# Linear attention on one core: q transposed by the DMA, k and q^T sharing their elementwise work, z from one-column products, two banks for kv

## Chip, cores, metric

One core of one Trainium2 chip. The metric is the device time of one execution in microseconds (us). "Span" is the time between the first and the last instruction of the profiled execution; it is about 2 us shorter than the device time. PE is the tensor engine, DVE the vector engine, ACT the scalar engine, POOL the GpSimd engine, and SP the engine that issues the DMAs.

## The reference

```python
B, H, S, D = 1, 32, 2048, 128          # q, k, v: bf16, normal * 0.05
phi_q = where(q > 0, q + 1, exp(q)) + 1e-6
phi_k = where(k > 0, k + 1, exp(k)) + 1e-6
kv  = einsum("bhsd,bhse->bhde", phi_k, v)
z   = einsum("bhsd->bhd", phi_k)
num = einsum("bhqd,bhde->bhqe", phi_q, kv)
den = einsum("bhqd,bhd->bhq", phi_q, z)[..., None] + 1e-6
out = num / den
```

Both kernels split phi(x) into two parts, min(exp(x), 1) + 1e-6 and max(x, 0), and let PE add them: two products instead of one. Each head is 512 KB of q, of k, of v and of output.

## The kernel before

All work is written as one list of operations per engine. Every engine runs its own list strictly in order and waits on semaphores for results of the others. So the order in which the helper functions are called in the main loop *is* the order on each engine. The parts that matter (cut):

```python
def T(h):      # PE: 16 transposes of q into PSUM, (L243)
def ek(h):     # ACT: exp of k                    (L190)
def eq(h):     # ACT: exp of q^T from PSUM        (L194)
def rqa(h):    # ACT: max(q^T, 0), half or all    (L202)
def rqb(h):    # DVE: the other half              (L207)
def emrk(h):   # DVE: min of exp(k) (L220), max of k (L222)
def emq(h):    # DVE: min of exp(q^T)             (L227)
def v1(h):     # POOL: copy v next to a column of ones (L236)
def kv(h):     # PE: 32 products of 129 columns; column 129 is z  (L251)
def kvs(h):    # ACT: copy kv to SBUF             (L215)
def nA(h), nC(h):   # PE: numerators and denominators, 12 + 4 tiles (L259, L263, L265)
def f(h, which):    # DVE: reciprocal (L293) and multiply (L299)
...
for i in range(NH):
    eq(i)
    ...
    rqa(i)
    kvs(i + 1)
    ek(i + 2)
    f(i - 1, "A")
    rqb(i)
    emq(i)
    f(i - 1, "C")
    emrk(i + 2)
    T(i + 1)
    nA(i)
    nC(i)
    kv(i + 2)
```

The loop is skewed. In iteration i, PE computes numerators of head i, while DVE divides those of head i-1. Neither waits for the whole of the other.

## Time and profile before

199.74 us (median of 2 runs, 199.07 to 200.41); span 197.3 us.

| engine | busy us | share of the span | us per head |
|---|---|---|---|
| PE | 170.6 | 86% | 5.3 |
| DVE | 161.6 | 82% | 5.05 |
| ACT | 160.0 | 81% | 5.0 |
| DMA | about 415 GB/s from 10 to 150 us | full there | 5.05 |

(Per head: the busy time, for PE, DVE and ACT, over 32. The DMA row: 2.1 MB at 415 GB/s.) Four resources lie within 7% of each other, so no share says which one limits.

From the chain of waits of the kernel before, in the middle of the span (start us, us, what):

```profile
84.71 0.28 ACT la L215
84.99 1.81 ACT la L190
86.80 0.02 issue
86.82 0.69 DVE la L220
...
88.30 1.76 DVE la L299
...
90.71 1.07 PE la L243 x16
...
93.75 1.99 PE la L251 x32
95.77 0.28 ACT la L215
```

The copy of kv comes back after 11.06 us and two heads (84.71 to 95.77): 5.53 us per head. In these two heads the chain passes through ACT, DVE and PE, each for a part of the time. The others overlap it.

One more view: two stretches of the start, with the busy time of each engine, then "PEclk", the granted clock of PE as a share of full speed, then DMA share and GB/s:

```profile
12.10:15.50 3.40, 0.00 (x0) 0.00 (x0) 1.29 (x3) 2.08 (x2) 1.65 (x1) 1.00 1.02 413
17.00:20.20 3.20, 3.20 (x34) 3.20 (x32) 0.00 (x0) 2.07 (x3) 1.71 (x1) 0.50 1.02 408
```

PE does nothing for 3.4 us, and from 17.0 us on it gets half its clock for 3.2 us, though it is then fully busy.

### The profile page before, as it was taken

Reading aid. Unit: us, or ns where it says so; the run is one execution under the profiler, and the core shown is the slowest. Engines: PE = TensorE matmul, PEld = TensorE weight load, DVE = VectorE, ACT = ScalarE, POOL = GpSimd, SP = SyncE. Lnnn points to the kernel's source line nnn. Section 1 sums busy time; section 2 is a strip of 40 time slices with the busy share of each in tenths; the row PEclk is TensorE's granted clock in tenths of the full one; section 3 lists DMA queues with packets and bytes.
Section 4 is the critical chain, followed back from the end, with each engine's and each line's share of the span. In section 5 each row is a group of like instructions: output and inputs, shape, how many; then the busy total and the mean of one; then the engine's idle time right before and its main releaser. Section 6 shows DMA issues by size and latency. Waiting matters only on the chain.

```text
span 197.3 us, 6384 instructions
## 1 busy us (share of the span) xinstructions
PE 170.6 (86%) x2842; PEld 160.5 (81%) x2842; DVE 161.6 (82%) x254; ACT 160.0 (81%) x129; POOL 68.4 (35%) x38
## 2 busy tenths in 40 slices
PE   6948999988898899988898889988898889988850
PEld 6938889888897889888897889888897889988850
DVE  0213899899989999899989999899989999899774
ACT  4563789988898889988898889988898889998530
POOL 1333343322344444332344444432344444431000
PEclk9997999999999999999999999999999999999985
DMA  6999999999999999999999999999999622222133
GB/s 228 346 418 411 412 404 407 410 404 416 416 411 422 412 416 419 411 420 414 414 420 413 419 418 414 419 414 417 416 415 394 246 116 110 106 106 105 61 130 137
DMA packets 18603, 67.52 MB, mean 342 GB/s; under 512 B 2064, under 2 KB 2192, under 8 KB 18576
## 3 DMA queue, kind: packets, MB, share of 16 engines
q1 hardware_dynamic: 18576, 67.12, 84.4%
q8 instruction: 22, 0.36, 0.7%
q14 instruction: 5, 0.04, 0.1%
HBM read 50.33 MB, written 16.78 MB: 340 GB/s over the span
## 4 chain that ended last, share of the span: by engine, by line
ACT 37%; PE 33%; DVE 22%; DMA 3%; issue 2%; POOL 1%; SPq 0%
ACT la L190 21%; PE la L251 18%; DVE la L299 9%; ACT la L202 6%; ACT la L194 6%; DVE la L220 6%; PE la L243 5%; PE la L263 5%; PE la L265 5%; DVE la L222 4%; DMA la<-in_v_dram 3%; ACT la L215 3%; DVE la L207 2%; DVE la L293 1%; POOL la L236 1%
## 5 line engine op out<-in xcount | busy, mean ns | idle before, releaser
L236 POOL TENSOR_SCALAR la<-la 128x2048 bf16<-128x2048 bf16 x32 | 67.7, 2116 | 109.1 <-PE la L265 97.5
L299 DVE TENSOR_TENSOR la<-la 128x1536 bf16<-128x1536 f32 x64 | 78.4, 1224 | 2.2
L251 PE MATMUL la<-la 128*128 128x129 bf16 x1024 | 65.3, 222 | 5.7 <-DVE la L222 5.4
L251 PEld LDWEIGHTS la<-la 128*128 128x128 bf16 x1024 | 59.7, 98 | 10.2 <-DVE la L222 7.1
L265 PE MATMUL la<-la 128*128 128x129 bf16 x512 | 66.7, 221 | 0.0
L263 PE MATMUL la<-la 128*128 128x129 bf16 x512 | 66.6, 220 | 0.0
L194 ACT ACTIVATE la<-la 128x2048 bf16<-128x2048 bf16 x32 | 59.8, 1869 | 3.7 <-PE la L243 3.7
L190 ACT ACTIVATE la<-la 128x2048 bf16<-128x2048 bf16 x32 | 60.9, 1902 | 1.9 <-DMA la<-in_k_dram 1.9
L265 PEld LDWEIGHTS la<-la 128*128 128x128 bf16 x512 | 49.8, 97 | 0.0
L263 PEld LDWEIGHTS la<-la 128*128 128x128 bf16 x512 | 47.6, 98 | 0.0
L243 PE MATMUL la<-la 128*128 128x128 bf16 x512 | 35.0, 222 | 12.7 <-DVE la L207 11.5
L220 DVE TENSOR_SCALAR la<-la 128x2048 bf16<-128x2048 bf16 x32 | 22.2, 694 | 27.4 <-ACT la L190 27.4
L243 PEld LDWEIGHTS la<-la 128*128 128x128 bf16 x512 | 29.6, 99 | 18.0 <-DVE la L207 15.5
L202 ACT ACTIVATE la<-la 128x1024 bf16<-128x1024 bf16 (+1 forms) x32 | 39.6, 1238 | 0.0
L259 PE MATMUL la<-la 128*128 128x3 bf16 (+1 forms) x192 | 32.5, 169 | 2.2 <-DVE la L227 2.2
L215 ACT ACTIVATE la<-la 128x129 bf16<-128x129 f32 x32 | 9.0, 280 | 23.0 <-PE la L251 23.0
L222 DVE TENSOR_SCALAR la<-la 128x2048 bf16<-128x2048 bf16 x32 | 22.0, 687 | 0.0
L227 DVE TENSOR_SCALAR la<-la 128x2048 bf16<-128x2048 bf16 x32 | 21.8, 683 | 0.0
L259 PEld LDWEIGHTS la<-la 128*128 128x128 bf16 x192 | 19.0, 99 | 2.4 <-DVE la L227 2.4
L207 DVE TENSOR_SCALAR la<-la 128x1024 bf16<-128x1024 bf16 x24 | 16.3, 681 | 0.0
L293 DVE RECIPROCAL la<-la 128x12 f32<-128x12 f32 x64 | 12.9, 201 | 2.5 <-PE la L265 2.5
L308 PE MATMUL la<-la 128*128 128x120 bf16 x90 | 7.6, 268 | 1.5 <-POOL la L149 1.5
(13 smaller groups left out, 9.9 us busy)
## 6 DMA issues: line engine op xcount, KB each, us to landing
la<-in_k_dram SPq DMA_DIRECT2D x32, 512.0 KB, 15.0
la<-in_q_dram SPq DMA_DIRECT2D x32, 512.0 KB, 15.0
la<-in_v_dram SPq DMA_DIRECT2D x32, 512.0 KB, 15.2
out_dram<-la SPq DMA_DIRECT2D x31, 512.0 KB, 15.1
out_dram<-la SPq DMA_DIRECT2D x1, 384.0 KB, 2.3
out_dram<-la SPq DMA_DIRECT2D x1, 128.0 KB, 2.1
```

Of the source, the lines that this page charges most:

```text
L190: add("ACT", f"ek{h}", lambda e: e.activation(em_sb[:, h % 2], k_sb[:, h % NI], ACT.Exp), [f"ldk{h}"] + ([f"kv{h - 2}"] if h >= 2 else []))
L194: add("ACT", f"eq{h}", lambda e: e.activation(emq_sb[:, h % 2], xT[:, :], ACT.Exp), [f"T{h}"] + ([f"nC{h - 2}"] if h >= 2 else []))
L202: add("ACT", f"rqa{h}", lambda e: e.activation(rq_sb[:, h % 2, 0:n], xT[:, 0:n], ACT.Relu), [f"T{h}"] + ([f"nC{h - 2}"] if h >= 2 else []))
L220: add("DVE", f"em{h}", lambda e: e.tensor_scalar(em_sb[:, s], em_sb[:, s], 1.0, EPS, op0=ALU.min, op1=ALU.add), [f"ek{h}"])
L222: add("DVE", f"rk{h}", lambda e: e.tensor_scalar(rk_sb[:, s], k_sb[:, h % NI], 0.0, None, op0=ALU.max), [f"ldk{h}"] + ([f"kv{h - 2}"] if h ...
L236: add("POOL", f"v1{h}", lambda e: e.tensor_scalar(v1_sb[:, h % 2, :, 0:D], v_sb[:, h % NI].rearrange("p (j d) -> p j d", d=D), 1.0, 0.0, o ...
L243: ins = e.transpose(xT[:, j * P:(j + 1) * P], q_sb[:, h % NI, j * D:(j + 1) * D], ident[:])
L251: ins = e.matmul(kv_ps, lhsT=src[:, h % 2, j * D:(j + 1) * D], rhs=v1_sb[:, h % 2, j, :], start=(j + part == 0), stop=(j == NT - 1 and par ...
L259: e.matmul(_ap(o_ps[:, :], slot(tiles[0]) + D, [[NC, n]]), lhsT=ones[:], rhs=epsr[:, 0:n], start=True, stop=False, skip_group_check=True)
L263: e.matmul(o, lhsT=emq_sb[:, s, t * P:(t + 1) * P], rhs=kvs_sb[:, s, :], start=False, stop=False, skip_group_check=True)
L265: ins = e.matmul(o, lhsT=rq_sb[:, s, t * P:(t + 1) * P], rhs=kvs_sb[:, s, :], start=False, stop=True, skip_group_check=True)
L299: add("DVE", f"f{which}{h}", lambda e: e.tensor_tensor(out=_ap(o_sb[:, :, :, :], ob + t0 * D, [[n * D, nb], [D, n], [1, D]]), in0=_ap(o_ps ...
```

## The change

The intent is to take work off each engine. The DMA delivers q already transposed, so PE has no transposes to do and ACT and DVE can treat k and q^T as one tile of 4096 columns. z comes from products of one column of ones, so POOL need not copy v. Two kv banks let the next kv begin before the last one is copied. The core of the diff (cut; renaming and bookkeeping left out):

```diff
-    NO = 6
-    LAG = 2
+    NE = 3
+    NO = 10
+    LAG = 8
...
-            load("q", q_sb, qf, h, ["T"])
+            add("SP", f"ldq{h}", lambda e: e.dma_start_transpose(
+                out=kq_sb[:, s, 1].rearrange("p (j d) -> p j d", d=D),
+                in_=qf[h].rearrange("(p j) d -> p (j d)", j=NT)), dep("eq", "rq"), dma=f"q{s}")
...
+        def exps(h):      # ACT: one exp over k and q^T (L194)
+        def relus(h):     # DVE: one max over both (L202)
+        def mins(h):      # DVE: one min over both (L207)
...
-                        ins = e.matmul(kv_ps, lhsT=src[...], rhs=v1_sb[:, h % 2, j, :], ...)
+                        e.matmul(o[:, 0:D], lhsT=w, rhs=v_sb[:, h % NI, j * D:(j + 1) * D], ...)
+                        ins = e.matmul(o[:, D:NC], lhsT=w, rhs=one1[:], start=False, ...)
...
         for i in range(NH):
-            (the skewed loop above)
+            if i + 2 < NH:
+                exps(i + 2)
+                relus(i + 2)
+            if i + 1 < NH:
+                kv(i + 1)
+                kvs(i + 1)
+            nA(i)
+            nC(i)
+            r(i)
+            f(i, "A")
+            f(i, "C")
+            if i + 2 < NH:
+                mins(i + 2)
```

NE is the number of buffers for the results of exp and max, NO that of output buffers, LAG the number of heads by which a store stands behind the loads in SP's list.

More of the change, by code (lines that the diff above doesn't have):

```diff
@@ L31, in add @@
             self.count[name] = self.count.get(name, 0) + (16 if dma is not None else 1)
-        if key is not None:
-            assert key not in self.where, key
+        for k in [] if key is None else key if isinstance(key, list) else [key]:
+            assert k not in self.where, k
             assert dma is not None or inc
-            self.where[key] = (name, self.count[name], eng, len(self.ops[eng]))
+            self.where[k] = (name, self.count[name], eng, len(self.ops[eng]))
         self.ops[eng].append((fn, tuple(deps), name, (16 if dma is not None else 1) if (dma is not None or inc) else 0))
@@ L124, in bass_standalone__linear_attn_elu__prompt_kernel, with kv_ps @@
         sb = lambda shape, dt=bf16: alloc(nc.sbuf_tensor, shape, dt)
-        k_sb, q_sb, v_sb = sb([P, NI, N]), sb([P, NI, N]), sb([P, NI, N])
-        em_sb, rk_sb = sb([P, 2, N]), sb([P, 2, N])
-        v1_sb = sb([P, 2, NT, NC])
-        emq_sb, rq_sb = sb([P, 2, N]), sb([P, 2, N])
+        kq_sb, v_sb = sb([P, NI, 2, N]), sb([P, NI, N])
+        em_sb, rk_sb = sb([P, NE, 2, N]), sb([P, NE, 2, N])
         kvs_sb = sb([P, 2, NC])
-        rden_sb = sb([P, 2, NT], fp32)
+        rden_sb = sb([P, 2, 18], fp32)
         o_sb = sb([P, NO, NT, D])
         ident, ones, epsr, one1 = sb([P, P]), sb([P, P]), sb([P, 3]), sb([P, 1])
-        xT = alloc(nc.psum_tensor, [P, N], bf16)
-        o_ps = alloc(nc.psum_tensor, [P, 6 * 512], fp32)
-        KV0 = 5 * 512 + 2 * NC
-        kv_ps = o_ps[:, KV0:KV0 + NC]
+        o_ps = alloc(nc.psum_tensor, [P, 8 * 512], fp32)
         CO = 4 * 512
+        def kv_ps(h):
+            o = (6 + h % 2) * 512
+            return o_ps[:, o:o + NC]
         def slot(t):
@@ L145, in bass_standalone__linear_attn_elu__prompt_kernel @@
         add = pr.add
-        add("POOL", "ident0", lambda g: g.memset(ident[:], 0.0))
-        add("POOL", "ident", lambda g: g.affine_select(
-            out=ident[:], in_=ident[:], compare_op=ALU.not_equal, fill=1.0, base=0, pattern=[[-1, P]],
-            channel_multiplier=1), ["ident0"])
+        add("POOL", "ident", lambda g: g.memset(ident[:], 1.0))
         ea, eb, ec = _eps_pieces()
@@ L156, in bass_standalone__linear_attn_elu__prompt_kernel @@
         add("DVE", "ones", lambda g: g.memset(ones[:], 1.0))
-        for s in range(2):
-            add("DVE", f"v1ones{s}", lambda g, s=s: g.memset(v1_sb[:, s, :, D:NC], 1.0))
-        def load(name, dst, src, h, freed):
-            dep = [f"{f}{h - NI}" for f in freed] if h >= NI else []
-            add("SP", f"ld{name}{h}", lambda e: e.dma_start(
-                dst[:, h % NI].rearrange("p (j d) -> p j d", d=D), rows(src, h)), dep, dma=f"{name}{h % NI}")
-        def loads(h):
-            load("k", k_sb, kf, h, ["ek", "rk"])
-            load("q", q_sb, qf, h, ["T"])
-            load("v", v_sb, vf, h, ["v1"])
+        add("DVE", "one1", lambda g: g.memset(one1[:], 1.0))
+        def loads(h):
+            s = h % NI
+            dep = lambda *f: [f"{x}{h - NI}" for x in f] if h >= NI else []
+            add("SP", f"ldk{h}", lambda e: e.dma_start(
+                kq_sb[:, s, 0].rearrange("p (j d) -> p j d", d=D), rows(kf, h)), dep("ek", "rk"), dma=f"k{s}")
+            add("SP", f"ldq{h}", lambda e: e.dma_start_transpose(
+                out=kq_sb[:, s, 1].rearrange("p (j d) -> p j d", d=D),
+                in_=qf[h].rearrange("(p j) d -> p (j d)", j=NT)), dep("eq", "rq"), dma=f"q{s}")
+            add("SP", f"ldv{h}", lambda e: e.dma_start(
+                v_sb[:, s].rearrange("p (j d) -> p j d", d=D), rows(vf, h)), dep("kv"), dma=f"v{s}")
         def store(h):
@@ L186, in bass_standalone__linear_attn_elu__prompt_kernel @@
                 store(h - LAG)
-        def ek(h):
-            add("ACT", f"ek{h}", lambda e: e.activation(em_sb[:, h % 2], k_sb[:, h % NI], ACT.Exp),
-                [f"ldk{h}"] + ([f"kv{h - 2}"] if h >= 2 else []))
-        def eq(h):
-            add("ACT", f"eq{h}", lambda e: e.activation(emq_sb[:, h % 2], xT[:, :], ACT.Exp),
-                [f"T{h}"] + ([f"nC{h - 2}"] if h >= 2 else []))
-        def split(h):
-            return h % 4 != 3
-        def rqa(h):
-            n = N // 2 if split(h) else N
-            add("ACT", f"rqa{h}", lambda e: e.activation(rq_sb[:, h % 2, 0:n], xT[:, 0:n], ACT.Relu),
-                [f"T{h}"] + ([f"nC{h - 2}"] if h >= 2 else []))
@@ L205, in rqb, with parts @@
-        def rqb(h):
-            if split(h):
-                add("DVE", f"rqb{h}", lambda e: e.tensor_scalar(
-                    rq_sb[:, h % 2, N // 2:], xT[:, N // 2:], 0.0, None, op0=ALU.max),
-                    [f"eq{h}"] + ([f"nC{h - 2}"] if h >= 2 else []))
-        def rqs(h):
-            return [f"rqa{h}"] + ([f"rqb{h}"] if split(h) else [])
+        def split(h):
+            return h == 0 or h == NH - 1
+        def parts(h):
+            return ((("k", 0, 1), ("q", 1, 2)) if split(h) else (("kq", 0, 2),))
@@ new lines, in exps @@
+        def exps(h):
+            for p, a, b in parts(h):
+                dep = [f"ld{c}{h}" for c in p]
+                if h >= NE:
+                    dep += [f"kv{h - NE}", f"nC{h - NE}"]
+                add("ACT", [f"e{c}{h}" for c in p], lambda e, a=a, b=b: e.activation(
+                    em_sb[:, h % NE, a:b], kq_sb[:, h % NI, a:b], ACT.Exp), dep)
+        def relus(h):
+            for p, a, b in parts(h):
+                dep = [f"ld{c}{h}" for c in p]
+                if h >= NE:
+                    dep += [f"kv{h - NE}", f"nC{h - NE}"]
+                add("DVE", [f"r{c}{h}" for c in p], lambda e, a=a, b=b: e.tensor_scalar(
+                    rk_sb[:, h % NE, a:b], kq_sb[:, h % NI, a:b], 0.0, None, op0=ALU.max), dep)
@@ L214, in kvs @@
+        def mins(h):
+            for p, a, b in parts(h):
+                add("DVE", [f"m{c}{h}" for c in p], lambda e, a=a, b=b: e.tensor_scalar(
+                    em_sb[:, h % NE, a:b], em_sb[:, h % NE, a:b], 1.0, EPS, op0=ALU.min, op1=ALU.add),
+                    [f"e{c}{h}" for c in p])
         def kvs(h):
-            add("ACT", f"kvs{h}", lambda e: e.activation(kvs_sb[:, h % 2], kv_ps, ACT.Copy),
+            add("ACT", f"kvs{h}", lambda e: e.activation(kvs_sb[:, h % 2], kv_ps(h), ACT.Copy),
@@ L216, in kvs @@
                 [f"kv{h}"] + ([f"nC{h - 2}"] if h >= 2 else []))
-        def emrk(h):
-            s = h % 2
-            add("DVE", f"em{h}", lambda e: e.tensor_scalar(
-                em_sb[:, s], em_sb[:, s], 1.0, EPS, op0=ALU.min, op1=ALU.add), [f"ek{h}"])
-            add("DVE", f"rk{h}", lambda e: e.tensor_scalar(
-                rk_sb[:, s], k_sb[:, h % NI], 0.0, None, op0=ALU.max), [f"ldk{h}"] + ([f"kv{h - 2}"] if h >= 2 else []))
-        def emq(h):
-            s = h % 2
-            add("DVE", f"emq{h}", lambda e: e.tensor_scalar(
-                emq_sb[:, s], emq_sb[:, s], 1.0, EPS, op0=ALU.min, op1=ALU.add), [f"eq{h}"])
@@ L230, in v1 @@
-        def v1(h):
-            dep = [f"ldv{h}"]
-            if h >= 2:
-                dep += [f"kv{h - 2}"]
-            if h >= 3:
-                dep += [f"nA{h - 3}"]
-            add("POOL", f"v1{h}", lambda e: e.tensor_scalar(
-                v1_sb[:, h % 2, :, 0:D], v_sb[:, h % NI].rearrange("p (j d) -> p j d", d=D), 1.0, 0.0,
-                op0=ALU.mult, op1=ALU.add), dep)
-        def T(h):
-            def f(e):
-                for j in range(NT):
-                    ins = e.transpose(xT[:, j * P:(j + 1) * P], q_sb[:, h % NI, j * D:(j + 1) * D], ident[:])
-                return ins
-            add("PE", f"T{h}", f, [f"ldq{h}", "ident"] + (([f"eq{h - 1}"] + rqs(h - 1)) if h else []))
@@ L247, in kv @@
         def kv(h):
             def f(e):
+                o = kv_ps(h)
                 for j in range(NT):
                     for part, src in ((0, em_sb), (1, rk_sb)):
-                        ins = e.matmul(kv_ps, lhsT=src[:, h % 2, j * D:(j + 1) * D], rhs=v1_sb[:, h % 2, j, :],
-                                       start=(j + part == 0), stop=(j == NT - 1 and part == 1))
-                return ins
-            add("PE", f"kv{h}", f, [f"em{h}", f"rk{h}", f"v1{h}", "v1ones0", "v1ones1"] + ([f"kvs{h - 1}"] if h else [])
-                + ([f"fC{h - 3}"] if h >= 3 else []))
@@ L257, in num @@
-        def num(h, tiles, bank, n, e):
-            s = h % 2
-            e.matmul(_ap(o_ps[:, :], slot(tiles[0]) + D, [[NC, n]]), lhsT=ones[:], rhs=epsr[:, 0:n], start=True, stop=False,
+                        w = src[:, h % NE, 0, j * D:(j + 1) * D]
+                        e.matmul(o[:, 0:D], lhsT=w, rhs=v_sb[:, h % NI, j * D:(j + 1) * D],
+                                 start=(j + part == 0), stop=(j == NT - 1 and part == 1), skip_group_check=True)
+                        ins = e.matmul(o[:, D:NC], lhsT=w, rhs=one1[:], start=False,
+                                       stop=(j == NT - 1 and part == 1), skip_group_check=True)
@@ L260, in num @@
+                return ins
+            add("PE", f"kv{h}", f, [f"mk{h}", f"rk{h}", f"ldv{h}", "one1"] + ([f"kvs{h - 2}"] if h >= 2 else []))
+        def num(h, tiles, bank, e):
+            s = h % NE
+            e.matmul(_ap(o_ps[:, :], 512 * bank + D, [[NC, 3]]), lhsT=ones[:], rhs=epsr[:, 0:3], start=True, stop=False,
                      skip_group_check=True)
@@ L262, in num @@
                 o = o_ps[:, slot(t):slot(t) + NC]
-                e.matmul(o, lhsT=emq_sb[:, s, t * P:(t + 1) * P], rhs=kvs_sb[:, s, :], start=False, stop=False,
+                e.matmul(o, lhsT=em_sb[:, s, 1, t * P:(t + 1) * P], rhs=kvs_sb[:, h % 2, :], start=False, stop=False,
                          skip_group_check=True)
-                ins = e.matmul(o, lhsT=rq_sb[:, s, t * P:(t + 1) * P], rhs=kvs_sb[:, s, :], start=False, stop=True,
+                ins = e.matmul(o, lhsT=rk_sb[:, s, 1, t * P:(t + 1) * P], rhs=kvs_sb[:, h % 2, :], start=False, stop=True,
                                skip_group_check=True)
@@ L271, in f @@
                 for b in range(4):
-                    ins = num(h, range(3 * b, 3 * b + 3), b, 3, e)
+                    ins = num(h, range(3 * b, 3 * b + 3), b, e)
                 return ins
-            add("PE", f"nA{h}", f, [f"emq{h}", f"kvs{h}", "ones", "eps0", "eps1", "eps2"] + rqs(h)
+            add("PE", f"nA{h}", f, [f"mq{h}", f"rq{h}", f"kvs{h}", "ones", "eps0", "eps1", "eps2"]
                 + ([f"fA{h - 1}"] if h else []))
@@ L278, in f, with r @@
             def f(e):
-                num(h, (12, 13), 4, 2, e)
-                return num(h, (14, 15), 5, 2, e)
-            add("PE", f"nC{h}", f, [f"nA{h}"][:0] + ([f"fC{h - 1}"] if h else [])
-                + ([f"kvs{h + 1}"] if h + 1 < NH else []))
+                num(h, (12, 13), 4, e)
+                return num(h, (14, 15), 5, e)
+            add("PE", f"nC{h}", f, [f"fC{h - 1}"] if h else [])
+        def r(h):
+            add("DVE", f"r{h}", lambda e: e.reciprocal(
+                rden_sb[:, h % 2].rearrange("p (a b) -> p a b", b=3),
+                _ap(o_ps[:, :], D, [[512, 6], [NC, 3]])), [f"nA{h}", f"nC{h}"])
         def f(h, which):
@@ L287, in f @@
             ob = o_sb[:, h % NO, 0, 0:1].offset - o_sb[:, :, :, :].offset
-            if which == "A":
-                t0, nb, n, base = 0, 4, 3, 0
-            else:
-                t0, nb, n, base = 12, 2, 2, CO
-            rb = rden_sb[:, s, t0:t0 + 1].offset - rden_sb[:, :, :].offset
-            add("DVE", f"r{which}{h}", lambda e: e.reciprocal(
-                rden_sb[:, s, t0:t0 + nb * n].rearrange("p (a b) -> p a b", b=n),
-                _ap(o_ps[:, :], base + D, [[512, nb], [NC, n]])), [f"n{which}{h}"] + ([f"kvs{h + 2}"] if which == "C" and h + 2 < NH else []))
-            dep = [f"r{which}{h}"]
+            t0, nb, n, base, r0 = (0, 4, 3, 0, 0) if which == "A" else (12, 2, 2, CO, 12)
+            rb = rden_sb[:, s, r0:r0 + 1].offset - rden_sb[:, :, :].offset
+            dep = [f"r{h}"]
             if h >= NO:
@@ L301, in f @@
                 in0=_ap(o_ps[:, :], base, [[512, nb], [NC, n], [1, D]]),
-                in1=_ap(rden_sb[:, :, :], rb, [[n, nb], [1, n], [0, D]]), op=ALU.mult), dep)
+                in1=_ap(rden_sb[:, :, :], rb, [[3, nb], [1, n], [0, D]]), op=ALU.mult), dep)
         def warm(n, col):
@@ L311, in warm @@
             add("PE", None, g, ["ident"], inc=False)
-        warm(60, 512 + 3 * NC)
-        for h in range(NH):
-            v1(h)
-        ek(0)
-        T(0)
-        warm(30, 512 + 3 * NC)
-        emrk(0)
+        warm(60, 512)
+        exps(0)
+        relus(0)
+        mins(0)
         kv(0)
+        kvs(0)
+        exps(1)
+        relus(1)
+        mins(1)
         for i in range(NH):
-            eq(i)
-            if i == 0 and NH > 1:
-                rqa(0)
-                kvs(0)
-                ek(1)
-                emrk(1)
-                kv(1)
-            else:
-                rqa(i)
+            if i + 2 < NH:
+                exps(i + 2)
+                relus(i + 2)
             if i + 1 < NH:
+                kv(i + 1)
                 kvs(i + 1)
-            if i + 2 < NH:
-                ek(i + 2)
-            if i >= 1:
-                f(i - 1, "A")
-            rqb(i)
-            emq(i)
-            if i >= 1:
-                f(i - 1, "C")
-            if i + 2 < NH:
-                emrk(i + 2)
-            if i + 1 < NH:
-                T(i + 1)
             nA(i)
             nC(i)
+            r(i)
+            f(i, "A")
+            f(i, "C")
             if i + 2 < NH:
-                kv(i + 2)
-        f(NH - 1, "A")
-        f(NH - 1, "C")
+                mins(i + 2)
         pr.resolve()
```

## The prediction

> **What bounds the kernel now.** No engine alone: busy shares are PE 86%, DVE 82%, ACT 81%, and in 30-160 us the DMA engines are also full (about 415 GB/s in the slices). In the chain of waits a kvs copy follows every 5.53 us (84.71, 90.24, 95.77), so a head costs 5.53 us; the chain hops ACT exp, DVE min and max, PE kv, copy. It works because the loop is skewed: PE has the transposes and numerators of one head, DVE the normalization of the one before.
>
> **What the change removes.** Transposes on PE (16 in 1.07 us per head), the relu from PSUM on ACT (1.0 or 1.9 us) and DVE, the POOL copy of v (2.1 us, off the chain). ACT falls to about 3.6 (exp of 4096 columns, scaled from 1.03 us at 1024 and 1.87 at 2048) + 0.28 us per head.
>
> **What it adds.** PE: 32 one-column products per head. The 2- and 3-column products of the trace move the next start by about 0.03 us, so kv grows from 2.0 to about 3.0 us; numerators stay at 2.1; PE 5.1 us per head, as before. DVE: 4096-column max and min are about 1.2 us each (0.6 start to start at 2048), reciprocal 0.27, multiplies 1.67 + 0.6: about 4.9, as before. The transposing load: the Trainium skill, "DMA: Bandwidth & Descriptors", § Latency and other measured facts, gives 261 to 400 GB/s, which would be 1.3-2.0 us for 512 KB (an estimate; no transposing load is in this trace). With plain loads at 1.26 us, a head moves in at most 5.8 us.
>
> **What goes wrong: the order.** DVE does, per iteration i: relu(i+2), reciprocal(i), both multiplies(i), min(i+2). PE does kv(i+1), numerators(i). kv(i+2) needs min(i+2), which stands behind multiplies(i), which need numerators(i), which stand behind kv(i+1). So PE idles through reciprocal, multiplies and min, and DVE has only the relu to do while PE works. The second kv bank can't help. One iteration is a serial loop: 0.2 (drain) + 0.27 + 1.67 + 0.6 + 1.2 = about 4.0 us without PE, then 5.1 us of PE: 9.1 us at full clock.
>
> **The clock.** Near 12.1-15.6 us PE idles 3.5 us in the trace, and the granted clock is 0.50 from 17.0 to 20.4; after 2.4 us idle near 188 us it is 0.50 again. The Trainium skill, "TensorE: Matmul & The Clock Gate", Part 1, describes free-running windows of 3.4 us; the trace's change points fit. At 0.50 the 129-column spacing is 0.108 us instead of 0.056. A 4 us hole in each iteration should drop the clock for about one window of three: the iteration becomes about 10.2 us.
>
> **Sum.** First numerators done near 23 us; 30 iterations of 10.2 = 306; last head about 10; about 2 more from span to device time: about 340 us. With full clock throughout 305; with half clock throughout about 395. All DMA, at 5.8 us per head, hides.
>
> **In the profile.** Period 9-10.5 us per head; PE busy about 50-60%, longest wait PE for the DVE min, 4 us each; DVE waiting for the numerators about 4 us per head; DVE and PE alternating in the chain with nearly all of the span, ACT and DMA nearly absent; granted clock between 0.6 and 0.9; ACT about 40%; DMA about 200 GB/s, never full after the prefetch.
>
> **What would make it wrong.** The one-column products might cost less (weights not reloaded: about 0.9 us less per head) or each 0.06 us (1 us more). A transposing load far slower than the skill says (over 6 us per head) would make DMA the limit. If the clock is kept, about 305. If I misread the order, about 180.
>
> Faster 3%, within 2% 2%, slower 95%. 340 us, range 300 to 375.

(A correction to its first paragraph: of the three copies that it dates, the middle one, at 90.24 us, was read from the timeline. The chain shows the other two.)

## More of the kernel before

From the profile page of the kernel before, the busy tenths of DMA in 40 equal slices of the span, and the DMA queue that carries the kernel's transfers (packets, MB, share of 16 engines' time):

```profile
DMA  6999999999999999999999999999999622222133
...
q1 hardware_dynamic: 18576, 67.12, 84.4%
```

## The result, and the profile after

345.04 us (344.94 to 345.14, 2 runs) against 199.74. The ratio is 1.733, 95% interval 1.707 to 1.759. Ratios here and below are the mean time of one kernel's fast runs over that of the other's fast runs of the same rounds, so they are not quite the ratio of the medians. Executions over 1.5% slower than the fastest of the same kernel are left out of the means.

From the page of the changed kernel: busy time, the slices of PE, of its granted clock and of DMA, the queue, and the chain by engine.

```profile
PE 209.6 (61%) x3324; PEld 203.6 (59%) x3324; DVE 157.8 (46%) x169; ACT 126.2 (37%) x67; POOL 0.4 (0%) x5
...
PE   7565555776555776555676555677555677555673
...
PEclk9568888886868886868886868886868886868876
DMA  8999999999999988886679897779896011111013
...
q1 hardware_dynamic: 80528, 67.12, 73.7%
...
PE 58%; DVE 21%; issue 14%; DMA 3%; SPq 1%; ACT 1%; DVEq 0%
```

DVE does slightly less than before (157.8 us against 161.6), ACT much less (126.2 against 160.0), and yet the time is 145 us longer. No engine is busy for more than 61% of the span. PE's own busy time rose, and its mean clock is below 0.9 in every slice but the first.

Who waited for whom in the changed kernel (us in total, times, longest):

```profile
DVE la L255 <- PE la L236: 166.8, 32, 5.7
...
PE la L221 <- DVE la L207: 121.3, 31, 5.1
```

The first line is the reciprocal waiting for the numerators, 5.2 us per head. The second is kv waiting for the min, 3.9 us per head. Two engines that wait for each other, for half and for a third of the span, are taking turns. The timeline of DVE shows one turn (start us, us, what; idle before, and what ended it):

```profile
158.87 0.27 DVE L255 RECIPROCAL la<-la 128x18 f32<-128x18 f32 x1 [5.60 <-PE la L236]
159.17 2.35 DVE L267 TENSOR_TENSOR la<-la 128x1536 bf16<-128x1536 f32 x2
161.45 1.22 DVE L207 TENSOR_SCALAR la<-la 128x4096 bf16<-128x4096 bf16 x1
162.58 1.22 DVE L202 TENSOR_SCALAR la<-la 128x4096 bf16<-128x4096 bf16 x1
168.88 0.27 DVE L255 RECIPROCAL la<-la 128x18 f32<-128x18 f32 x1 [5.08 <-PE la L236]
```

The min (L207) stands behind the multiplies (L267). PE's next line starts at 162.72 us, right after it:

```profile
158.61 0.22 PE L236 MATMUL la<-la 128*128 128x129 bf16 x1
162.72 0.23 PE L221 MATMUL la<-la 128*128 128x128 bf16 x1 [3.89 <-DVE la L207]
```

Over 29 iterations (reciprocals at 26.48 and 322.48 us) the period is 10.21 us per head. Stretches of 3.41 us laid side by side show the clock (columns as above: PE, PEld, DVE, ACT, POOL busy, then PEclk, DMA share, GB/s):

```profile
146.77:150.19 3.42, 1.53 (x29) 1.35 (x26) 1.82 (x2) 1.77 (x1) 0.00 (x0) 1.00 0.92 266
150.19:153.60 3.41, 1.41 (x22) 1.42 (x23) 3.07 (x4) 1.84 (x1) 0.00 (x0) 0.50 1.13 330
153.60:157.01 3.41, 3.41 (x53) 3.41 (x52) 0.00 (x0) 0.28 (x1) 0.00 (x0) 0.50 0.10 23
157.01:160.43 3.42, 1.82 (x34) 1.64 (x32) 1.53 (x2) 1.48 (x1) 0.00 (x0) 1.00 0.79 212
160.43:163.84 3.41, 1.12 (x27) 1.12 (x28) 3.37 (x4) 2.14 (x1) 0.00 (x0) 1.00 1.08 337
163.84:167.25 3.41, 3.41 (x52) 3.41 (x50) 0.00 (x0) 0.28 (x1) 0.00 (x0) 0.50 0.31 70
```

The stretches in which PE works without a pause run at half clock; both shown here follow a stretch in which PE was mostly idle. With the whole span laid out in such stretches (100 of them; the clock is 0.50 or 1.00 in each), all 38 in which PE was busy for less than 1.54 us were followed by half clock, and 48 of the 50 with more than 1.6 us by full clock. In this trace, then, the clock of a stretch follows from the work in the one before. The page "TensorE: Matmul & The Clock Gate" of the Trainium skill, Part 1, describes free-running windows of 3413 ns; that the clock is exactly 0.50 or 1.00 in each of these stretches agrees with it.

### The profile page after: what moved, and what is told of

Its sections match the earlier page's. It is cut to its first block, busy times and chain, and to the rows that moved or that the text cites. A ratio compares the mean times of both kernels' runs of the same rounds, so it can differ in the third digit from the quotient of the medians.

```text
span 343.2 us, 7188 instructions
## 1 busy us (share of the span) xinstructions
PE 209.6 (61%) x3324; PEld 203.6 (59%) x3324; DVE 157.8 (46%) x169; ACT 126.2 (37%) x67; POOL 0.4 (0%) x5
## 3 DMA queue, kind: packets, MB, share of 16 engines
q1 hardware_dynamic: 80528, 67.12, 73.7%
## 4 chain that ended last, share of the span: by engine, by line
PE 58%; DVE 21%; issue 14%; DMA 3%; SPq 1%; ACT 1%; DVEq 0%
PE la L221 35%; PE la L234 12%; PE la L236 10%; DVE la L207 10%; DVE la L267 8%; DMA la<-in_q_dram 3%; DVE la L255 3%; ACT la L194 1%; PE la L223 1%; SPq L160 1%; PE la L230 1%; SPq L158 0%; DVEq L114 0%; SPq L163 0%
## 5 line engine op out<-in xcount | busy, mean ns | idle before, releaser
L221 PE MATMUL la<-la 128*128 128x128 bf16 x1024 | 126.4, 254 | 125.0 <-DVE la L207 121.3
L221 PEld LDWEIGHTS la<-la 128*128 128x128 bf16 x1024 | 120.7, 134 | 130.5 <-DVE la L207 126.6
L194 ACT ACTIVATE la<-la 128x4096 bf16<-128x4096 bf16 (+1 forms) x34 | 116.0, 3416 | 65.8 <-PE la L236 62.4
L223 PE MATMUL la<-la 128*128 128x1 bf16 x1024 | 124.3, 198 | 0.0
L223 PEld LDWEIGHTS la<-la 128*128 128x128 bf16 x1024 | 101.0, 103 | 0.0
L255 DVE RECIPROCAL la<-la 128x18 f32<-128x18 f32 x32 | 8.7, 271 | 166.8 <-PE la L236 166.8
L234 PE MATMUL la<-la 128*128 128x129 bf16 x512 | 78.5, 239 | 0.0
L236 PE MATMUL la<-la 128*128 128x129 bf16 x512 | 78.3, 243 | 0.0
L267 DVE TENSOR_TENSOR la<-la 128x1536 bf16<-128x1536 f32 x64 | 75.4, 1219 | 1.1
L236 PEld LDWEIGHTS la<-la 128*128 128x128 bf16 x512 | 54.5, 107 | 0.0
L234 PEld LDWEIGHTS la<-la 128*128 128x128 bf16 x512 | 53.7, 110 | 0.0
L202 DVE TENSOR_SCALAR la<-la 128x4096 bf16<-128x4096 bf16 (+1 forms) x34 | 39.3, 1159 | 10.7 <-DMA la<-in_q_dram 7.7
L207 DVE TENSOR_SCALAR la<-la 128x4096 bf16<-128x4096 bf16 (+1 forms) x34 | 39.2, 1155 | 3.1 <-ACT la L194 3.1
L230 PE MATMUL la<-la 128*128 128x3 bf16 x192 | 33.5, 175 | 2.2 <-DVE la L267 2.2
L230 PEld LDWEIGHTS la<-la 128*128 128x128 bf16 x192 | 22.1, 115 | 2.3 <-DVE la L267 2.3
L275 PE MATMUL la<-la 128*128 128x120 bf16 x60 | 6.1, 304 | 1.0 <-POOL la L147 1.0
L275 PEld LDWEIGHTS la<-la 128*128 128x128 bf16 x60 | 5.9, 149 | 1.0 <-POOL la L147 1.0
```

What stands on the lines that cost most here:

```text
L194: add("ACT", [f"e{c}{h}" for c in p], lambda e, a=a, b=b: e.activation(em_sb[:, h % NE, a:b], kq_sb[:, h % NI, a:b], ACT.Exp), dep)
L202: add("DVE", [f"r{c}{h}" for c in p], lambda e, a=a, b=b: e.tensor_scalar(rk_sb[:, h % NE, a:b], kq_sb[:, h % NI, a:b], 0.0, None, op0=ALU ...
L207: add("DVE", [f"m{c}{h}" for c in p], lambda e, a=a, b=b: e.tensor_scalar(em_sb[:, h % NE, a:b], em_sb[:, h % NE, a:b], 1.0, EPS, op0=ALU. ...
L221: e.matmul(o[:, 0:D], lhsT=w, rhs=v_sb[:, h % NI, j * D:(j + 1) * D], start=(j + part == 0), stop=(j == NT - 1 and part == 1), skip_group_ ...
L223: ins = e.matmul(o[:, D:NC], lhsT=w, rhs=one1[:], start=False, stop=(j == NT - 1 and part == 1), skip_group_check=True)
L230: e.matmul(_ap(o_ps[:, :], 512 * bank + D, [[NC, 3]]), lhsT=ones[:], rhs=epsr[:, 0:3], start=True, stop=False, skip_group_check=True)
```

## The experiments

The theory, called the *order theory* below: the loss is a serial loop, numerators on PE, then reciprocal, multiplies and min on DVE, then kv on PE, made longer by the clock that the pauses cost. The rivals: the transposing loads set the time; the one-column products do. Every experiment below is an edit of the changed kernel, or of e1 or e2 where it says so, except the last, which edits the kernel before. Each was timed in three rounds beside the kernel before. The medians given are of all its runs, slow ones too; where two kernels are subtracted, the means of the fast runs are used if they differ from the medians by more than 0.3%. The changed kernel itself was not timed again in these rounds, so differences of 1% from it are not read. The record calls the verdicts of e1 to e4 unclear (three of eight runs of the kernel before were slow there), though the 95% intervals of all four ratios lie clear of 1, for e2 0.922 to 0.935.

A caution on "right result": q is so small that phi_q is near 1 everywhere, and the output hardly depends on it. The comparison with the reference also passed three kernels in which q was deliberately *not* transposed (e2, e3 and e7). So here it says little about q, and a pass is not evidence for the transposing path.

### e1: the min before the divisions

```diff
             nA(i)
             nC(i)
+            if i + 2 < NH:
+                mins(i + 2)
             r(i)
             f(i, "A")
             f(i, "C")
-            if i + 2 < NH:
-                mins(i + 2)
```

> The changed kernel with one move: the DVE min of head i+2 stands before the reciprocal and multiplies of head i, so PE's next kv no longer waits for them. Order theory (the loss is the serial loop PE, then DVE, then PE): the hole of 3.9 us per iteration closes, PE, DVE and ACT overlap, a head needs about 5.1 us of engine time, the granted clock goes back near 1.0, and the time falls by more than 100 us. The trace of the change shows k, q transposed and v going out every 5.6 us in the prefetch, so the loads may then be the limit: 205 to 235 us. Rival (the transposing loads already set the time): no gain, 330 to 345 us. Rival (one-column products): no gain either, since all of them stay.

Measured: 258.81 us (255.5 to 260.52), ratio 1.295 to the kernel before. (Its profile fell in a run, 260.52 us, 2% above its fastest run; it is used for counts, and no difference of a few per cent is read from it.) The three fast runs have a mean of 257.7 us. Moving one call took 345.0 - 257.7 = 87 us away, so the order was most of the loss. But the range of 205 to 235 was missed by 24 us. The DMA queue on e1's page:

```profile
q1 hardware_dynamic: 80528, 67.12, 97.8%
```

Its waits:

```profile
ACT la L194 <- PE la L236: 89.1, 19, 22.6
DVE la L267 <- DMA out_dram<-la: 62.3, 16, 22.0
...
PE la L221 <- DVE la L207: 19.9, 17, 6.8
```

The wait of kv for the min fell from 121.3 to 19.9 us. In its place DVE waits for stores to free output buffers, and the DMA queue is busy for 97.8% of the span. The DMA has become the limit.

### e2: the same, with q loaded by a plain DMA

```diff
-            add("SP", f"ldq{h}", lambda e: e.dma_start_transpose(
-                out=kq_sb[:, s, 1].rearrange("p (j d) -> p j d", d=D),
-                in_=qf[h].rearrange("(p j) d -> p (j d)", j=NT)), ...)
+            add("SP", f"ldq{h}", lambda e: e.dma_start(
+                kq_sb[:, s, 1].rearrange("p (j d) -> p j d", d=D), rows(qf, h)), ...)
```

> As e1, and q is loaded by a plain DMA into the same place (wrong result on purpose: q is not transposed). If e1 is then limited by the transposing loads, this falls to the engine work: about 5.2 us per head, 175 to 195 us. If e1 is limited by PE or DVE, e2 equals e1 within 2%.

Measured: 184.82 us (184.01 to 185.59), ratio 0.928. It computes something else, so it is no candidate. But it splits the account: with the order mended, the transposing loads cost 257.7 - 184.8 = 73 us. Its queue line:

```profile
q1 hardware_dynamic: 18576, 67.12, 91.3%
```

The share times the span is the time of all 16 DMA engines. For the same 67.12 MB:

| kernel | share x span | us of 16 engines |
|---|---|---|
| before | 0.844 x 197.3 | 166.5 |
| e2, plain q | 0.913 x 183.0 | 167.1 |
| changed | 0.737 x 343.2 | 252.9 |
| e1 | 0.978 x 258.7 | 253.0 |

A plain load or store of 512 KB takes 166.5 / 128 = 1.30 us. A transposing load takes (252.9 - 166.5) / 32 = 2.70 us more, so 4.0 us, or 131 GB/s. That is an estimate that charges the whole difference to the transposing loads, and a mean over the run, not a fixed price. The same product is 182 us for e3 below, whose loads are all plain, and 268 us for e4, so it holds to about 10%. And in the first 100 us of the changed kernel, before any store, 12 heads of k, q^T and v went out in 5.60 us each at a DMA share of 1.08 (18.78 to 86.02 us): less two plain loads, that leaves 3.0 to 3.5 us for the transposing load.

### e3: plain q, order as changed

The same replacement as in e2, applied to the changed kernel.

> The changed kernel, its order kept, with q loaded by a plain DMA (wrong result on purpose). Order theory: the loop does not wait for loads after the first heads, so only the start gains, some 3 to 8 us: 336 to 343 us. Rival (transposing loads set the time): falls to below 250 us.

Measured: 342.05 us (340.73 to 343.15), ratio 1.720. The transposing loads are not what makes the changed kernel slow. Their cost is there (252.9 us of DMA work), but it hides under a loop of 10.2 us per head.

### e4: dummy products in the hole

```diff
             nA(i)
             nC(i)
+            if i + 1 < NH:
+                warm(66, (6 + i % 2) * 512 + 256)   # 66 products of 120 columns, into a part of a kv bank that nobody reads
             r(i)
```

> The changed kernel, its order kept, with 66 dummy products on PE in the hole after each head's numerators (about 3.4 us, shorter than the hole of 3.9 us; they write a part of a kv bank that nobody reads). It separates the clock's share: if the dropped clock costs about 1.1 us per iteration as predicted, the granted clock is near 1.0 throughout, the period falls from 10.2 to about 9.1 us, and the time to 300 to 315 us, though PE does more work. If the clock costs nothing, 345 us or more.

Measured: 296.51 us (295.6 to 297.17), ratio 1.489. PE does 66 more products per head, and the kernel is 48.5 us faster. The granted clock is 0.98 instead of 0.77. The period is 8.63 us (reciprocals at 102.98 and 197.95, 11 iterations). Two of the reciprocals on its DVE timeline:

```profile
102.98 0.27 DVE L255 RECIPROCAL la<-la 128x18 f32<-128x18 f32 x1 [3.70 <-PE la L236]
...
197.95 0.27 DVE L255 RECIPROCAL la<-la 128x18 f32<-128x18 f32 x1 [3.69 <-PE la L236]
```

So the clock cost 10.21 - 8.63 = 1.58 us per iteration, more than the 1.1 us predicted, and the loop without it is 8.63 us, not 9.1.

### e6: two one-column products per head instead of 32

```diff
-                        ins = e.matmul(o[:, D:NC], lhsT=w, rhs=one1[:], start=False, ...)
+                        if j == NT - 1:
+                            ins = e.matmul(o[:, D:NC], lhsT=w, rhs=one1[:], start=False, ...)
```

> The changed kernel, its order kept, with 2 one-column products per head instead of 32 (wrong result on purpose: z is too small). Order theory: they are a term of the burst, 30 x 0.03 = 0.9 us of 5.1 us, and the hole of 3.9 us stays; with the clock dropping for a part of each loop the period goes from 10.2 to 9.2-10.0 us: 305 to 335 us. Rival (the one-column products are what makes the change slow): falls to about 200 us.

Measured: 341.76 us (341.21 to 344.0), ratio 1.708; the result is wrong, as intended. The rival falls: these products do not make the change slow. But the range of 305 to 335 was missed too. Work of almost 0.8 us per head was taken away, and only 3 us came back in all, which is within 1%. Three reciprocals of its DVE timeline:

```profile
104.12 0.27 DVE L256 RECIPROCAL la<-la 128x18 f32<-128x18 f32 x1 [5.31 <-PE la L237]
...
114.37 0.27 DVE L256 RECIPROCAL la<-la 128x18 f32<-128x18 f32 x1 [5.32 <-PE la L237]
...
124.60 0.27 DVE L256 RECIPROCAL la<-la 128x18 f32<-128x18 f32 x1 [5.31 <-PE la L237]
```

The steps are 10.25 and 10.23 us, 10.24 on average, which is three windows of 3.413 us; and the mean clock of the run fell to 0.686, from 0.774. A new theory: the loop is locked to the clock's windows, and what is saved is given back as more time at half clock. The changed kernel fits it too. Its steps are uneven (10.01 to 10.61 us), but from 138.32 us on they repeat every five heads, at 189.51, 240.72 and 291.91 us: 51.2 us, which is 15 windows, again 10.24 us per head. (The 10.21 us above includes the start, before the pattern sets in.) The next run tests whether the saving was eaten by the clock.

### e10: dummies and few one-column products

The edits of e4 and of e6 together.

> Dummy products in the hole as in e4 and 2 one-column products per head as in e6 (wrong result on purpose). e6 took 0.9 us of PE work per head away and gained only 3 us in all. Theory: the loop was held at three windows of the clock (10.24 us), and what was saved was given back as a longer time at half clock. With the clock held up by the dummies, the same removal must show: 30 x 0.03 x 32 = about 27 us under e4's 296.5, so 265 to 278 us. Rival (the one-column products cost next to nothing in any case): 290 to 297 us.

Measured: 277.58 us (274.14 to 280.27), ratio 1.383. Two of the four runs were slow; the fast ones have a mean of 275.1 us. With the clock held at 0.98, the same removal gains 296.5 - 275.1 = 21.4 us, where without the dummies it gained 3.3. So the saving is real on PE and was eaten by the clock. That it was eaten by a lock to whole windows fits the periods, but no run tested it apart. The gain is smaller than the 27 us foreseen. A one-column product costs less than 0.03 us: most periods of e10 are 7.87 us against 8.63, and (8.63 - 7.87) / 30 is 0.025 us. And twice DVE waited for a store to free an output buffer, 3.0 us in all: at this pace the DMA begins to show.

### e5: one kv bank

```diff
-            o = (6 + h % 2) * 512
+            o = 6 * 512
...
-  ... + ([f"kvs{h - 2}"] if h >= 2 else []))
+  ... + ([f"kvs{h - 1}"] if h >= 1 else []))
```

> The changed kernel with one kv bank instead of two (right result). Order theory: the copy of kv (0.28 us) is long done before the next kv starts, so the second bank gives nothing here: 341 to 349 us, equal to the changed kernel's 345. If the two banks did matter, clearly slower.

Measured: 344.47 us (344.36 to 344.72), ratio 1.716. The second bank gives nothing in this order. PE waits for the min, and the copy of kv is over long before that.

### e7: plain q in 256-byte pieces

```diff
-                kq_sb[:, s, 1].rearrange("p (j d) -> p j d", d=D), rows(qf, h)), ...)
+                kq_sb[:, s, 1].rearrange("p (j d) -> p j d", d=D),
+                qf[h].rearrange("(j p) d -> p j d", j=NT)), ...)
```

(an edit of e2)

> As e2 (min first, q loaded by a plain DMA, wrong result on purpose), but q moves in 256-byte pieces instead of 4 KB rows, as small as the packets that the transposing load shows (66,000 packets under 512 B more than before). If the small packets are what makes a transposing load cost 4.0 us of all 16 DMA engines instead of 1.3, this is as slow as e1, 250 to 260 us. If it is the transposing itself, it is much nearer to e2's 185: 185 to 210 us.

Measured: 233.39 us (231.82 to 234.9), ratio 1.165: between the two ranges, so neither reason alone. Its queue:

```profile
q1 hardware_dynamic: 80016, 67.12, 99.1%
```

0.991 x 230.0 = 227.9 us of 16 engines, so a plain load in 256-byte pieces takes 1.30 + (227.9 - 166.5) / 32 = 3.2 us. Of the 2.7 us that a transposing load costs more than a plain one, 1.9 us also appear with small pieces and no transposing. The remaining 0.8 us is left to the transposing itself. The 25 us between e7 and e1 stand in the device times too. But the sum is argued from two kernels; that the two causes simply add was not shown.

### e8: k, v and stores from POOL, only q from SP

```diff
-            add("SP", f"ldk{h}", ...
+            add("POOL", f"ldk{h}", ...
(the same for ldv and the stores; an edit of e1)
```

> As e1 (min first, right result), with k, v and the stores issued from POOL, which is idle, so that SP issues nothing but the transposing loads (4.6 us each on SP in e1). If a transposing load only blocks the queue behind it while the DMA engines have room, k, v and stores flow beside it and the time falls towards 185-200 us. If it really occupies the 16 engines for 4.0 us, the sum of DMA work stays at about 253 us and the time at 245 to 265 us.

Measured: 333.13 us (319.31 to 350.41; runs too uneven for a ratio, and the profile fell in a slow run). Both expectations were wrong. The DMA queue of SP in its timeline:

```profile
91.71 49.37 SPq L160 DMA_TRANSPOSE la<-in_q_dram  x3
```

Three transposing loads took 49 us to issue, 16 us each, where e1 has mostly 4.5 to 6 us, and ACT then waits 178 us in total for q^T, against 22.9 us in e1. The plain transfers were slow as well: POOL's loads took 15 us from issue to landing, against about 5 us in e1, and from 82.7 to 154 us the engines moved only 124 to 199 GB/s. Why both are slow is open. The Trainium skill, "DMA: Bandwidth & Descriptors", § Queues, rings and completion order, says that a DMA engine goes round the queues that have work, packet by packet; that alone does not explain why the total falls, and no run here tests it. The run also changed more than the number of streams: the profile lists POOL's queue as software_dynamic and SP's as hardware_dynamic.

### e9: q transposed as one matrix of 2048 by 128

```diff
-                out=kq_sb[:, s, 1].rearrange("p (j d) -> p j d", d=D),
-                in_=qf[h].rearrange("(p j) d -> p (j d)", j=NT)), ...)
+                out=kq_sb[:, s, 1], in_=qf[h]), ...)
...
-                e.matmul(o, lhsT=em_sb[:, s, 1, t * P:(t + 1) * P], ...)
+                e.matmul(o, lhsT=em_sb[:, s, 1].rearrange("p (m j) -> p j m", j=NT)[:, t, :], ...)
(the same for rk_sb; an edit of e1)
```

> As e1 (min first, right result), with q transposed as one flat matrix of 2048 rows by 128 columns instead of 128 rows of 16 blocks; PE then reads the stationary operand of the numerators with a step of 16 elements. If the cost of a transposing load lies in its reading pattern (rows 4 KB apart), this is faster, 190 to 230 us; if it lies in the transposing, 250 to 265 us. If strided weights load more slowly, the numerator spacing rises above 0.056 us.

Measured: 260.79 us (259.81 to 263.34), ratio 1.304, the same as e1 within 1%. The reading pattern in HBM is not the cause. The weight loads with a step of 16 elements took 150 to 156 ns instead of 107 to 110 in e1, and the product spacing rose to 0.062 us. That does not count here, since the DMA is the limit.

### e11: stores two heads behind instead of eight

```diff
-    LAG = 8
+    LAG = 2
(an edit of e1)
```

> As e1 (min first, right result) with stores issued 2 heads behind the loads instead of 8. In e1 DVE stood up to 22 us before a free output buffer, because the first store stands on SP behind 16 heads of slow loads. If the DMA work itself is the limit (253 us of all 16 engines), the stall was a symptom: 250 to 260 us. If the late stores were the limit, 205 to 235 us.

Measured: 252.03 us (248.31 to 257.42), ratio 1.244. The long waits for stores are gone. Instead ACT waits for q^T. Its queue, and the longest of its waits:

```profile
q1 hardware_dynamic: 80528, 67.12, 106.1%
```

```profile
ACT la L194 <- DMA la<-in_q_dram: 93.8, 30, 6.4
```

So e1's stall was mostly a symptom; the work of the DMA is the limit. (The fast runs, 248.31 and 251.21 us, are 3% below those of e1, so the late stores cost little. A share above 100% says that packets of different transfers overlap in this count, so the 253 us of the table is not an exact floor.)

### e12: transposing load for every fourth head, in the kernel before

```diff
+        def bydma(h):
+            return h % 4 == 3
(those heads: q loaded by dma_start_transpose; no T(h); eq(h) reads q_sb; the max is one DVE instruction from q_sb, none on ACT)
```

> The kernel before, with the transposing load for every fourth head only: those heads have no transposes on PE, their exp reads SBUF, and their relu runs on DVE from SBUF instead of 1.9 us on ACT. DMA work, worked out from the traces: 166.5 + 8 x 2.7 = 188 us. PE saves 1.07 us and ACT 1.9 us per four heads. Theory (the transposing load costs more DMA time than it saves on the engines once DMA is near full): 194 to 204 us, no gain beyond 2%. Rival (a small dose pays): 185 to 193 us.

Measured: 211.44 us (208.38 to 213.32), ratio 1.042: slower than before, and slower than the range. Even a quarter of the heads does not pay. In this mixed stream a transposing load holds SP for 14 us (65.15 to 79.76 us in its timeline, 0.4 to 0.5 us for most of the plain ones around it), and everything behind it in SP's list waits. But the engines are not idle in that time: up to 77 us they move 418 GB/s, which is the plain transfers issued before. What is lost comes after: from 77 to 84 us they move 201 GB/s, so such a load costs about 3.6 us of full rate (an estimate: 7 x (1 - 201/418)). The two fast runs, 208.38 and 209.92 us, are 9 us above the kernel before. The edit also moved the max of these heads from ACT to DVE, whose busy time rose from 161.6 to 166.2 us; that share was not separated. The estimate of 188 us counted only the DMA's work. The count in the profile, taken in a run marked slow, is 0.948 x 211.5 = 200.5 us.

No correct version faster than the kernel before was found.

## Why the prediction was right

The time (340 predicted, 345.04 measured) and its cause were right. Point by point:

- **The serial loop: right.** e1 moved one call and took 87 us away; e3, e5 and e6 changed the loads, the banks and the one-column products and moved the time by at most 1%.
- **The hole of 4.0 us: right.** PE waits 121.3 / 31 = 3.9 us for the min.
- **The work of PE, 5.1 us at full clock: too large by about half a microsecond.** e4's period of 8.63 us, less 3.9 us, leaves 4.7. The mis-sized term is kv: in e4, at full clock, 2.60 us pass from its first product to the first of the numerators (124.08 to 126.68 us), where 3.0 was forecast. The one-column product, 0.025 us instead of 0.03, is less than half of that; the rest is in the 128-column products, since kv in e10, almost without one-column products, takes 1.85 us where the forecast had 2.0.
- **The clock, 10.2 - 9.1 = 1.1 us per iteration: too small.** It is 1.58 us (e4). The forecast had the clock drop for about one window of three; it is half in 45 of the 100 stretches. The two errors cancelled to a period of 10.21 us, and that the number came out so close is partly luck. e6 and e10 suggest why the total was nevertheless robust: with these pauses the loop settles at three clock windows per head, 10.24 us, and some tenths of PE work more or less hardly show. The prediction did not foresee this.
- **"All DMA, at 5.8 us per head, hides": it hid, at a wrong size.** The page "DMA: Bandwidth & Descriptors" of the Trainium skill, § Latency and other measured facts, gives a bandwidth from which the prediction estimated 1.3 to 2.0 us for the transposing load; here it is about 4.0 us over the run. A head then moves in 3 x 1.3 + 4.0 = 7.9 us, still less than 10.2. Had the order been good, this term would have decided the result.
- **"If I misread the order, about 180": wrong for that reason.** e1 is the kernel with the order right, and takes 259 us. Only with plain loads (e2) is it 185.
- **The signs in the profile:** period 10.21 us (9 to 10.5 said), PE busy 61% (50 to 60), clock 0.77 (0.6 to 0.9), ACT 37% (40), DMA 197 GB/s over the span (200): right or nearly so. DVE waited 5.2 us per head for the numerators, not 4. "Never full after the prefetch" was wrong, or the prefetch far longer than meant: DMA shows 8 or 9 tenths in each of the first 18 slices, 154 us.

Where the 145 us come from, then: e1 shows that with the order alone mended 87 us go, down to the limit that the transposing loads set. These loads keep the mended kernel 58 us above the kernel before. Without either (e2), 185 us would be possible, but that kernel lacks the transposed q.

## What to carry to other kernels

Before merging or moving instructions, write each engine's list in order and follow one value around the loop; if engine A's next step stands behind B's work on A's current step, the two engines take turns, and their times add up, however low the shares become. When PE gets pauses of a few microseconds per iteration, ask what its clock does: here dummy products in the pauses were worth 48 us, and saved work was worth almost nothing until they were there. Work moved to the DMA needs a measured price too: the pair e1 and e2, the order mended with and without the transposing load, shows the second obstacle. The same replacement under the bad order (e3) does not show it.

## What the Trainium skill lacked or had wrong

- "DMA: Bandwidth & Descriptors", § Latency and other measured facts, gives 261 GB/s (non-contiguous middle dimension) and about 350-400 GB/s (contiguous) for a transposing load, and "Advanced Engine Details and Errata", § X-Bar Transpose (TRN2), says they "are as fast as regular DMAs". Here, among plain transfers that keep the engines full, a 512 KB transposing load costs about 4.0 us of all 16 engines as a mean over the run, 131 GB/s, against 1.30 us for a plain one (both estimates from the busy shares; 3.0 to 3.5 us before the first store); reading it as one contiguous matrix changed nothing (e9, 260.79 against 258.81 us).
- The same DMA page, § Why small descriptors are slow (HBM only), works out 27% of overhead for 256-byte descriptors, besides descriptor metadata. A plain load in 256-byte pieces took 3.2 us instead of 1.3 (e7).
- No page says what a transposing load costs beside other traffic. Beside POOL's transfers (e8) each held SP for 16 us, against mostly 4.5 to 6 in e1, and the plain transfers slowed too. Among plain loads and stores (e12) the engines moved 201 GB/s for 7 us around one, against 418 just before.
- "TensorE: Matmul & The Clock Gate", Part 1, has the windows, the half clock and loops that fall back to it in each iteration, but not that such a loop can settle at a whole number of windows: 10.24 us per head in e6, and 51.2 us per five heads in the changed kernel, which has 0.8 us of PE work more per head. It asks for an idle window; in the changed kernel's trace, stretches in which PE was busy for 1.12, 1.41 and 1.53 us of 3.41 were already followed by half clock, and one with 1.82 us by the full clock.
